# DeltaNet and expert layers on one core: first expert layer in 64-column tiles, and twelve unread products

## The chip, the core and the metric

The kernel runs on one core of one Trainium2 chip. The metric is the device time of one execution in microseconds, lower is better. [...] PEld is TensorE's weight load, DVE is VectorE, ACT ScalarE, POOL GpSimd, SP SyncE.

## What is computed

A DeltaNet recurrence over 4 batches, 8 heads and 768 steps of 48 values gives 3072 rows of 384 values. A gate gives each row one of 8 experts; each expert keeps its 80 rows of largest gate weight and sends them through two layers. The part around the change:

```python
logits = x @ w_gate                      # x: 3072 x 384, 8 experts
expert_idx = np.argmax(logits, axis=1)
...
for e in range(E):
    tok_idx = np.where(expert_idx == e)[0]
    if len(tok_idx) > capacity:          # capacity 80
        gw = gate_w[tok_idx]
        tok_idx = tok_idx[np.argpartition(-gw, capacity)[:capacity]]
    h = np.maximum(x[tok_idx] @ w1[e], 0.0)          # 384 -> 1024
    out[tok_idx] = gate_w[tok_idx, None] * (h @ w2[e])   # 1024 -> 384
```

Everything is float32, apart from a few bfloat16 helpers.

## The kernel before

The recurrence is cut into 12 chunks of 64 steps. For each chunk c a hand-written order runs on all engines: transposes of keys and queries (both), Gram products (gram), the inverse of a triangular matrix (solve, spread, merge_p2 to merge_y5), the state's chain (chain_ks, chain_tr, chain_qs, chain_ku, chain_pu), the transposes of the chunk's output rows (out_t, L500) and the gate's logits (logits, L510). Nearly all its products go through the helper mm (L207), so the profile shows them on one line and the tiles tell them apart: SB,KQ is chain_ks and chain_qs, R,Y chain_tr, UB,PT chain_pu, S_ps chain_ku, XB,B merge_p2. The products of chain_ks and merge_p2 take 128 rows by 64 columns of weights, and consecutive ones write the lower and the upper 64 partitions of the same PSUM tile in turn. The products with identb and eyes at L374 (128x128 weights, 512 columns of bfloat16) begin each merge_p2.

Behind the last chunk VectorE finds the 80 best rows of each expert (L598 to L837), helped by a few products, and writes the row numbers idx_g. GpSimd then gathers each expert's rows (gather, L849) into xgs[e], 80 rows by 384.

The expert part is plain code without a hand-written order: the framework's scheduler sets the order of its instructions on each engine, and it may set some of them among those of the recurrence's last chunks. For each expert e:

- tokens_in(e) (L858, L860) turns the gathered rows with three transposes into xTs[e], 128 x 3 x 80.
- First layer (L873): 8 blocks f of 128 hidden values, each the sum of 3 products over c, with 128x128 weights from w1_t and the 80 columns of xTs[e]. Four blocks share a PSUM tile hp; when its 12 products are done, ScalarE writes Relu of it into hT (L876).
- The next expert's tokens_in.
- Second layer (L881): 8 products of 128x80 weights from hT with 384 columns of w2_t, summed in yp.
- VectorE scales yp by the gate weight (L884), GpSimd scatters the rows to the output (L885).

A float32 product leaves two records in the trace, a transpose or a bfloat16 product one. Ten weight tiles (load_w, L152) are in SBUF at once, those of experts 0 to 4; expert e's two buffers are filled again for expert e + 5 when they come free.

## Time and profile before

| | |
|---|---|
| median of 3 runs | 464.94 us (463.93 to 469.27) |
| the profiled execution | 462.81 us |
| its span in the trace | 461.1 us |
| PE busy | 348.5 us (76% of the span) |
| PEld busy | 298.0 us (65%) |
| DVE, ACT, POOL busy | 234.1, 118.4, 167.0 us |
| L873, first expert layer, PE busy | 48.9 us, 384 records |
| L881, second expert layer, PE busy | 43.8 us, 128 records |

Times inside the profile are microseconds from the span's start. A busy PE counts overlapping records once; the distance between the starts of two groups tells how long the first one held the engine. The mean of one record is its latency, longer than its share of the engine. The recurrence ends at about 310 us, the choice of rows at about 358, the expert part runs from 363.6 us.

### The profile page before, as it was taken

What the parts mean: (1) busy time and instruction counts of PE and PEld (TensorE: products, weight loads), DVE (VectorE), ACT (ScalarE), POOL (GpSimd) and SP (SyncE); (2) the same over time, 40 slices, a digit from 0 to 9 for tenths busy, and PEclk for the clock granted to TensorE, in tenths of its full rate; (3) what the DMA queues carried; (4) which work ended last, traced back from release to release, by engine and by line L of the source; (5) the groups of instructions that cost most, each with busy time, mean ns of one, the idle gap of its engine ahead of it and who ended that gap; (6) DMA issues with size and microseconds to landing.
All of it is one profiled execution on the core that took longest, in us unless ns stands there. A gap on an engine that the chain in (4) does not pass through costs nothing. (4 is left out here: it accounts for less than half of the span.)

```text
span 461.1 us, 16603 instructions
## 1 busy us (share of the span) xinstructions
PE 348.5 (76%) x7239; PEld 298.0 (65%) x7239; DVE 234.1 (51%) x620; ACT 118.4 (26%) x208; POOL 167.0 (36%) x414
## 2 busy tenths in 40 slices
PE   2781688889898979897899998860002499999995
PEld 2671577688787878886788887750001477777773
DVE  6999861733646464765824864278598100110000
ACT  3410224424534353343352423510000000000000
POOL 5771170377374828581837341011000600011000
PEclk9975687999999999899999999995555569999999
DMA  9691566584857576774747345128399638940000
GB/s 156 121 180 35 100 111 129 84 192 82 190 106 171 106 170 124 156 157 84 163 77 178 51 115 118 43 86 302 125 372 414 240 129 278 300 162 12 21 12 11
DMA packets 183592, 65.30 MB, mean 142 GB/s; under 512 B 165568, under 2 KB 176832, under 8 KB 183520
## 3 DMA queue, kind: packets, MB, share of 16 engines
q1 hardware_dynamic: 135552, 54.36, 46.0%
q10 hardware_dynamic: 47200, 7.91, 9.4%
q0 software_dynamic: 768, 1.97, 1.4%
q8 instruction: 57, 0.93, 0.8%
q14 instruction: 15, 0.12, 0.1%
HBM read 44.35 MB, written 19.86 MB: 139 GB/s over the span
## 5 line engine op out<-in xcount | busy, mean ns | idle before, releaser
L873 PEld LDWEIGHTS hp<-xTe,w 128*128 128x128 f32 x384 | 48.9, 210 | 2.5 <-issue 1.5
L873 PE MATMUL hp<-xTe,w 128*128 128x80 f32 x384 | 48.9, 293 | 0.1
L345 POOL TENSOR_TENSOR tmpTrue<-XY,NT 128x14 f32<-128x14 f32 (+6 forms) x140 | 39.9, 285 | 11.0
L881 PE MATMUL yp<-w,hT 128*80 128x384 f32 x128 | 43.8, 497 | 0.0
L876 ACT ACTIVATE hT<-hp 128x320 f32<-128x320 f32 x16 | 7.0, 437 | 135.4 <-PE hp L873 135.4
L340 POOL TENSOR_TENSOR XY<-NT,eye 128x256 f32<-128x256 f32 x10 | 8.5, 853 | 91.2 <-DMA NT<-a_blocks 91.2
L347 POOL TENSOR_TENSOR XY<-XY,tmpTrue 128x14 f32<-128x14 f32 (+6 forms) x140 | 37.3, 266 | 11.0
L885 POOL DMA_INDIRECT out_dram<-y,idx_s x8 | 7.4, 920 | 81.7 <-DVE y L884 81.7
L207 PE MATMUL pm<-SB,KQ 128*64 128x96 f32 x704 | 34.6, 252 | 1.9 <-DVE lg L512 1.7
L303 ACT COPY KQ<-pm 128x512 f32<-128x512 f32 x48 | 24.9, 612 | 33.7 <-DMA a_blocks<-B 20.5
L454 DVE TENSOR_TENSOR UB<-pm,beta_t 64x768 f32<-64x768 f32 x24 | 22.9, 955 | 20.1 <-PE pm L207 19.8
L884 DVE TENSOR_SCALAR y<-yp,gw_t 80x384 f32<-80x384 f32 x8 | 4.9, 614 | 55.0 <-PE yp L881 55.0
L207 PEld LDWEIGHTS pm<-SB,KQ 128*64 128x64 f32 x704 | 30.7, 139 | 2.9 <-PE pm L591 2.0
L881 PEld LDWEIGHTS yp<-w,hT 128*80 128x80 f32 x128 | 19.1, 154 | 20.1 <-issue 20.1
L381 DVE TENSOR_TENSOR P<-pm,mask 128x512 f32<-128x512 f32 x24 | 15.4, 682 | 31.0 <-PE pm L207 31.0
L207 PE MATMUL pm<-KQ 48*64 48x128 f32 x768 | 25.8, 285 | 5.7 <-ACT KQ L303 3.8
L207 PE MATMUL pm<-YB,P 128*64 128x128 f32 x384 | 25.7, 288 | 3.4 <-issue 3.4
L207 PEld LDWEIGHTS pm<-KQ 48*64 48x64 f32 x768 | 22.3, 140 | 8.5 <-ACT KQ L303 4.8
L207 PEld LDWEIGHTS pm<-XB,B 128*64 128x64 f32 x384 | 22.3, 144 | 8.2 <-issue 7.7
L207 PE MATMUL pm<-XB,B 128*64 128x128 f32 x384 | 25.3, 288 | 2.6 <-DMA XB<-inv_blocks 2.6
L476 ACT COPY SB<-S_ps 48x768 f32<-48x768 f32 x22 | 17.4, 793 | 30.9 <-PE S_ps L207 30.7
L207 PEld LDWEIGHTS pm<-YB,P 128*64 128x64 f32 x384 | 22.4, 143 | 4.2 <-issue 3.6
(169 smaller groups left out, 648.5 us busy)
## 6 DMA issues: line engine op xcount, KB each, us to landing
w<-in_moe_w_dram SPq DMA_DIRECT2D x16, 1536.0 KB, 7.0
a_blocks<-B ACTq DMA_DIRECT2D x24, 256.0 KB, 4.8
qn<-in_q_dram SPq DMA_DIRECT2D x24, 192.0 KB, 5.1
vin<-in_v_dram SPq DMA_DIRECT2D x24, 192.0 KB, 6.0
x_rows<-x SPq DMA_DIRECT2D x24, 192.0 KB, 2.7
out_dram<-zero SPq DMA_DIRECT2D x12, 384.0 KB, 4.3
kr<-in_k_dram SPq DMA_DIRECT2D x23, 192.0 KB, 4.5
inv_blocks<-XY SPq DMA_DIRECT2D x12, 256.0 KB, 4.5
```

The source lines that it names most:

```text
L207: nc.tensor.matmul(out, lhsT=lhsT, rhs=rhs, start=not acc, stop=not acc, skip_group_check=True)
L303: nc.scalar.copy(KQs[c][:, 4 * h : 4 * h + 4, n, :], pt[:, h].rearrange("r (g w) -> r g w", w=128))
L340: eng.tensor_tensor(out=X, in0=NT.rearrange("p s t -> p t s"), in1=eye16, op=Alu.add)
L345: eng.tensor_tensor(out=tv, in0=X[:, t + 1 :, t : t + 1].to_broadcast(sh), in1=NT[:, 0:t, t].unsqueeze(1).to_broadcast(sh), op=Alu.mult)
L347: eng.tensor_tensor(out=X[:, t + 1 :, 0:t], in0=X[:, t + 1 :, 0:t], in1=tv, op=Alu.add)
L381: nc.vector.tensor_tensor(out=P2[:, p].rearrange("r g e w -> r (g e) w"), in0=ps[:, p].rearrange("r (g w) -> r g w", w=64), in1=mask.unsqu ...
L454: nc.vector.tensor_tensor(out=UB[hs(e), :, e].rearrange("r (g c) d -> r c g d", c=2), in0=ps[hs(e), :, : 8 * D].rearrange("r c (g d) -> r ...
L476: nc.scalar.copy(SB[hs(p, D), :, :, p].rearrange("r (b g) e d -> r b (g e) d", b=2), S_ps[hs(p, D), :, : 8 * D].rearrange("r b (g d) -> r ...
L873: nc.tensor.matmul(hp[:, (f - f0) * cap : (f - f0 + 1) * cap], lhsT=w1_t[:, c, f * 128 : (f + 1) * 128], rhs=xTs[e][:, c, :], start=(c == ...
L876: nc.scalar.activation(hT[:, f0:f1, :], hp[:, : (f1 - f0) * cap].rearrange("p (f t) -> p f t", t=cap), Act.Relu)
L881: nc.tensor.matmul(yp[:cap, :DM], lhsT=hT[:, f, :], rhs=w2_t[:, f, :], start=(f == 0), stop=(f == FK - 1))
L885: nc.gpsimd.indirect_dma_start(out=out[:, :], out_offset=bass.IndirectOffsetOnAxis(ap=idx_s[:, e : e + 1], axis=0), in_=y[:, :], element_o ...
```

## The change

The first layer's products are cut in two: each block of 128 hidden values is now two products with 64 columns of weights, one for the lower and one for the upper 64 partitions of hp, in turn, with the same 80 columns of tokens. The arithmetic is the same. And between the gathers and tokens_in(0) stand twelve products of identb with eyes, 512 columns of bfloat16, into a PSUM tile of the pool ps_y that nothing reads.

```diff
     for e in range(E):
         gather(e)
+    wm = ps_y.tile([128, 512], F32, name="yp")
+    for _ in range(12):
+        nc.tensor.matmul(wm, lhsT=identb, rhs=eyes.rearrange("r g w -> r (g w)"), start=True, stop=True)
     tokens_in(0)
     for e in range(E):
         w1_t, w2_t = w_t[2 * e], w_t[2 * e + 1]
...
             for f in range(f0, f1):
                 for c in range(DK):
-                    nc.tensor.matmul(hp[:, (f - f0) * cap : (f - f0 + 1) * cap],
-                                     lhsT=w1_t[:, c, f * 128 : (f + 1) * 128], rhs=xTs[e][:, c, :],
-                                     start=(c == 0), stop=(c == DK - 1))
+                    for n in range(2):
+                        r = slice(64 * n, 64 * n + 64)
+                        nc.tensor.matmul(hp[r, (f - f0) * cap : (f - f0 + 1) * cap],
+                                         lhsT=w1_t[:, c, f * 128 + 64 * n : f * 128 + 64 * n + 64], rhs=xTs[e][:, c, :],
+                                         start=(c == 0), stop=(c == DK - 1), skip_group_check=True)
```

Three lines are added above it, so in the changed kernel the unread products are L866, the first layer L878, the second L886.

On PE, at the end of the recurrence (L510 are the logits of chunk 10, the two groups of L207 chain_ks and chain_tr of chunk 11), the difference of the two orders reads, from the last of the first six unread products on:

```order
+L866 LDWEIGHTS identb
+L866 MATMUL yp<-eyes,identb 128x512
 L510 MATMUL pm<-wg,xT 64x8 x12
 L591 MATMUL pm<-ident,ohg 48x128
 L207 MATMUL pm<-SB,KQ 64x96 x16
-L207 MATMUL pm<-R,Y 64x48 x32
+L866 LDWEIGHTS identb
+L866 MATMUL yp<-eyes,identb 128x512
```

Six unread products stand between L500 of chunk 10 and L510, four behind chain_ks, then one product with R, two unread products, and the other 31 with R. None stands behind these.

On PE, where the choice of rows ends (L825) and the experts begin, before the change:

```order
L825 MATMUL acc<-rhs,hot 80x40
L858 MATMUL xp<-ident,xg 128x80 x6
L873 MATMUL hp<-xTe,w_5718 128x80 x24
L881 MATMUL yp<-w_5720,hT 80x384 x8
L873 MATMUL hp<-xTe,w_5722 128x80 x24
L858 MATMUL xp<-ident,xg 128x80 x3
L881 MATMUL yp<-w_5724,hT 80x384 x8
```

The same place now:

```order
L825 MATMUL acc<-rhs,hot 80x40
L858 MATMUL xp<-ident,xg 128x80 x6
L878 MATMUL hp<-xTe,w_5718 64x80 x48
L886 MATMUL yp<-w_5720,hT 80x384 x8
L878 MATMUL hp<-xTe,w_5722 64x80 x48
L858 MATMUL xp<-ident,xg 128x80 x3
L886 MATMUL yp<-w_5724,hT 80x384 x8
```

The first layer has 48 products of 64 columns of weights where 24 of 128 stood; between L825 and L858 nothing was added. The order on the other engines is the same as before.

## Rows read from the trace of the kernel before

**Rows 1.** Page, the span in 40 equal slices, busy tenths.

```profile
PE   2781688889898979897899998860002499999995
PEclk9975687999999999899999999995555569999999
```

**Rows 2.** Order of time on PE, expert part: start, busy us, group of records.

```profile
364.73 10.53 PE L873 MATMUL hp<-xTe,w 128*128 128x80 f32 x48
375.05 6.54 PE L881 MATMUL yp<-w,hT 128*80 128x384 f32 x16
381.43 5.48 PE L873 MATMUL hp<-xTe,w 128*128 128x80 f32 x48
386.75 0.37 PE L858 MATMUL xp<-ident,xg 80*128 80x80 f32 x3
386.96 5.33 PE L881 MATMUL yp<-w,hT 128*80 128x384 f32 x16
392.12 5.48 PE L873 MATMUL hp<-xTe,w 128*128 128x80 f32 x48
...
450.88 5.33 PE L881 MATMUL yp<-w,hT 128*80 128x384 f32 x16
```

**Rows 3.** Costliest groups, expert part: count, busy us, mean ns, idle before.

```profile
L873 PEld LDWEIGHTS hp<-xTe,w 128*128 128x128 f32 x384 | 48.9, 210 | 2.5 <-issue 1.5
L873 PE MATMUL hp<-xTe,w 128*128 128x80 f32 x384 | 48.9, 293 | 0.1
...
L876 ACT ACTIVATE hT<-hp 128x320 f32<-128x320 f32 x16 | 7.0, 437 | 135.4 <-PE hp L873 135.4
```

**Rows 4.** Order of time on PE, recurrence at full clock.

```profile
278.33 0.61 PE L374 MATMUL pm<-eyes,identb 128*128 128x512 bf16 x2
278.87 1.97 PE L207 MATMUL pm<-XB,B 128*64 128x128 f32 x32
280.77 0.88 PE L500 MATMUL pm<-ident,x 128*128 128x128 f32 x6
...
283.30 1.52 PE L207 MATMUL pm<-SB,KQ 128*64 128x96 f32 x32
284.75 1.14 PE L207 MATMUL pm<-P,YB 64*64 64x32 f32 x64
```

**Rows 5.** Stretches in which the granted clock rises (PEclk behind the engines).

```profile
52.00:54.00 2.00, 1.37 (x14) 0.98 (x10) 1.76 (x9) 2.00 (x5) 0.00 (x0) 0.69 0.72 68
...
76.00:78.00 2.00, 2.00 (x20) 1.78 (x18) 0.00 (x0) 1.13 (x3) 0.00 (x0) 0.72 0.02 8
...
377.00:378.00 1.00, 1.00 (x4) 0.50 (x3) 0.00 (x0) 0.00 (x0) 0.00 (x0) 0.75 0.79 250
```

**Rows 6.** Order of time on PE, the groups ahead of the first two rises.

```profile
49.70 3.67 PE L207 MATMUL pm<-XB,B 128*64 128x128 f32 x32 [2.02 <-DMA XB<-inv_blocks]
...
71.44 2.80 PE L207 MATMUL S_ps<-UB,kn 128*48 128x96 f32 x32 [2.11 <-DVE UB L454]
73.99 2.81 PE L207 MATMUL pm<-UB,PT 128*64 128x96 f32 x32
```

**Rows 7.** Order of time, PE and DVE, end of chunk 10 and chunk 11.

```profile
296.32 0.88 PE L500 MATMUL pm<-ident,x 128*128 128x128 f32 x6
...
298.34 0.87 PE L510 MATMUL pm<-wg,xT 128*64 128x8 f32 x24 [1.15 <-ACT xT L502]
...
299.37 1.54 PE L207 MATMUL pm<-SB,KQ 128*64 128x96 f32 x32
...
301.57 0.31 PE L207 MATMUL pm<-R,Y 64*64 64x48 f32 x2 [0.66 <-DVE R L442]
...
303.23 1.94 DVE L454 TENSOR_TENSOR UB<-pm,beta_t 64x768 f32<-64x768 f32 x2 [1.25 <-PE pm L207]
```

**Rows 8.** Stretches: PE, PEld, DVE, ACT, POOL busy, clock, DMA share, GB/s.

```profile
310.00:320.00 10.00, 0.10 (x5) 0.04 (x1) 8.68 (x40) 0.00 (x0) 0.84 (x3) 0.63 0.79 274
...
371.00:372.00 1.00, 1.00 (x6) 1.00 (x6) 0.00 (x0) 0.00 (x0) 0.00 (x0) 0.50 0.00 0
```

## The prediction

> **What bounds the kernel now.** I read the page's slices first [rows 1]. TensorE is busy for nine tenths or more of slices 33 to 39 (11.5 us each), behind a gap, and its granted clock is 0.5 from slice 28 into slice 33 (the mean of 0.63 at 310 to 320 us puts the fall at 312.6 [rows 8]). [...] Then the order of time on PE [rows 2]: an expert is 48 records of the first layer (L873; each float32 product leaves two records), 3 transposes for the next expert, 16 records of the second layer (L881), and the next begins at once: 392.12 - 381.43 = 10.69 us each. The last group ends at 450.88 + 5.33 = 456.2 us, then 4.9 us of scaling, scatter and closing follow, which the change leaves alone. No PE group of rows 2 shows idle time before it, so what PE saves here goes to the end one for one.

> At full clock the first layer takes 386.75 - 381.43 = 5.32 us, 110.8 ns a record, the second 392.12 - 386.96 = 5.16 us, 322 ns a record of 384 columns, 0.84 ns a column. By that the 80 columns of a first-layer record need 67 ns. They take 110.8 because weight loads are the limit: the load row has the same 48.9 us busy as the product row [rows 3].

> **First layer in two 64-column tiles.** 384 records become 768, with the same 80 columns against half the weights. The trace has this form: 128x64 weights, columns of float32, consecutive products alternating between the two halves of the output partitions (merge_p2, chain_ks). There [rows 4] 32 records of 128 columns take 280.77 - 278.87 = 1.90 us, 32 of 96 columns 284.75 - 283.30 = 1.45 us: 0.44 ns a column and record, half the 0.84 of one tile (0.42). So the two tiles do stream side by side, and the loads lie under the streams. With 0.42 a column, the 96-column group leaves 1.45 - 32 x 96 x 0.00042 = 0.16 us over. If that is paid once a group, an expert's 96 records take 96 x 80 x 0.00042 + 0.16 = 3.39 us; if it is paid by record (5 ns), 3.71. I take 3.5, since the 128-column group leaves about the same 0.18 over. Bounds: 3.23 with nothing over, and 96 x 45.3 = 4.35 us if a record with 80 columns costs what one with 96 does. Gain: 5.32 - 3.5 = 1.82 us in each of experts 1 to 7, 12.7 us.

> [...]

> What hides the rest: ScalarE's Relu of the second half, 437 ns [rows 3], is needed only by the fifth product of the second layer, behind the transposes and four products (0.2 and 2.6 us), so it isn't late; without that cover it would cost half a us an expert. Weights: no DMA moves anything at 371 us [rows 8], so the ten tiles of experts 0 to 4 are in; the other six are issued when a buffer comes free, five experts before they are read, some 44 us ahead at the new pace. They aren't late next either; one that were would cost PE its remaining flight.

> **Expert 0 and the clock.** It takes 381.43 - 364.73 = 16.70 us now, 10.32 for the first layer, all at 0.5, and 6.38 for the second. The clock rose at 377.5 [rows 5], 2.4 us after the second layer began; 10.3 us of L873 before it had not raised it. What raised it elsewhere [rows 5, 6]: a group of 128x64 tiles from 49.70 on (rise at 53.2, 3.5 us later), and two such groups, of 48 and 64 columns, from 71.44 on (rise at 77.1, 5.7 us later). The new first layer has the form of these groups, so I expect the rise inside it, from 3.5 us after its start to its end at 6.4; between the two rows lies 4.6, and I take 4.7. At the half clock a record of 96 columns took 2.55 us / 32 = 80 ns (from 71.44 to the next group at 73.99 [rows 6], and 0.84 x 96 = 81); with 80 columns 67 ns. So 4.7 us hold 70 records, the other 26 take 0.95 us at 36.5 ns: 5.65, then 5.16 for the second layer at full clock. 16.70 - 10.81 = 5.9 us gained.

> **The twelve unread products.** They do not run while the rows come: the order places them ahead of that, six between the transposes of chunk 10 (L500) and its logits (L510), four behind chunk 11's first products (SB,KQ), two behind the first product with R. Ahead of the experts PE waits as it did, and the clock, which fell at 312.6 with the recurrence over, is not held up by products at 297 to 303 us. What they cost: two of the same shape took 278.87 - 278.33 = 0.54 us with the change of tiling [rows 4], 0.27 each at most. Now [rows 7]: PE is done with L500 at 297.2; six take 1.6 us, to 298.8, where L510 began at 298.34: 0.5 late. The SB,KQ group starts 0.5 late and takes 1.45; four more take 1.1 us, while the first R product waited until 2.20 after SB,KQ's start: 0.3 late. Two more take 0.5 where the wait for the second R was already under way: 0.2 to 0.4 late. Sum of the small delays 0.9 to 1.2; with the products at 0.22 (512 columns at half of 0.84, bfloat16 streaming at twice float32's rate) about 0.6. I take 0.8. Bounds: 0.3, and all of it, 12 x 0.27 = 3.2. Behind the waiting R product stand chunk 11's remaining products and, on VectorE, UB at 303.23, from which VectorE works on with hardly a gap (8.68 of 10 us at 310 to 320 [rows 8]) to the indices of the gather. So this delay moves the whole end.

> **Sum.** 12.7 + 5.9 - 0.8 = 17.8 us off the profiled execution's 462.81 (span 461.1 and 1.7 around it): 445.0. The median of the runs shown is 464.94, 2.1 more than the profiled one; I go half way, and forecast **446.0 us**.

> **Rivals.**
> 1. The clock rises only with the second layer, as now. For: in 10.3 us of L873 it didn't. Against: rows 6. Then 96 x 67 ns = 6.4 and 6.38 us, 2.0 more: 448.0.
> 2. The products cost their whole length, 3.2 instead of 0.8, because each change of tiling adds to them. For: three stretches in the middle of 64-column groups. Against: two of them stand where PE waited anyway. 448.4.
> 3. A record of 80 columns costs what one of 96 does, 45.3 ns. For: no row has 80 columns. 4.35 us an expert, 0.97 x 7 = 6.8 us; expert 0 gains 5.1 (59 records of 80 ns, 37 of 45.3, and 5.16); with -0.8 that is 11.1: 452.8.
> 4. [...] A 64-column load is 110.8 / 2 = 55.4 ns, a stream 67 ns; in series on each of two tiles 61 ns a record, 5.88 us an expert: 7 x 0.56 = 3.9 lost, 1.4 more in expert 0 (11.8 us at the half clock, no early rise), 0.8 for the products: 470.0. It decides from 55 ns a record at full clock. Against: rows 4 (59 ns with 128 columns, where the series would be 81), and L873 itself, whose 110.8 already hides a 67 ns stream.

> [...]

> **How the numbers follow.** Forecast 0.63, rival 1 0.13, rival 2 0.07, rival 3 0.10: all faster by over 1%, 0.93. A record of 53 to 55 ns, between rivals 3 and 4, would end within 1% (about what a measurement of this kernel can tell from no change): 0.03. Rival 4: 0.04. The range reaches from 442.5 (3.3 us an expert, 14.1 in seven; rise after 3.5 us, 6.5; products at 0.3: 20.3 us off the profiled execution, with no addition for the median) to 453.5, which takes in rivals 1 to 3.

> **What would show it.** Right: in the order of time, first-layer groups of 96 records, 3.4 to 3.7 us to the next group; experts 8.9 us apart; the granted clock rising inside the first group of the new tiles, before the second layer; the products at 297 to 303 us, UB of chunk 11 about 0.8 us later, and the gather's start later by the same. Wrong: groups of over 5.3 us (rival 4), a first group of 6.4 us at 0.5 throughout (rival 1), UB 3 us late (rival 2), experts more than 9.6 us apart (rival 3), or PE idle before a second layer, waiting for Relu or weights, which I have priced at nothing.

## The result, and the profile after

| | before | after |
|---|---|---|
| median | 465.42 us (463.93 to 469.27, 4 runs) | 448.47 us (445.92 to 448.77, 4 runs) |
| profiled execution | 462.81 us | 448.49 us |
| its span | 461.1 us | 446.7 us |

The ratio is 0.9611, with a 95% interval from 0.9543 to 0.968: faster, 2.5 us above the forecast of 446.0 and inside the range. The experiments further down ran beside runs of the kernel before on the same chip (17, 7 and 11); the 17 spread from 461.7 to 471.2 us, so parts of a microsecond are read from the traces and not from the times. Medians are of all executions; ratios leave out the slow ones, those more than 1.5% above the fastest of the same kernel (one of the 11 took 708 us).

The two lines of the page that answer to [rows 1], in 40 slices of now 11.2 us (PE is TensorE; PEclk is its granted clock in tenths of full speed, which stands at 0.5 or at 1.0 in the traces of before and after, a slice with both showing the mean):

```profile
PE   2752696889898989888979989897000148999995
PEclk9976688999999989999999999899555559999999
```

The low stretch of the clock is still there, over 5 slices instead of 5 and a part, and the dense end behind it is shorter. The order of time on PE in the expert part, against [rows 2] (start, busy us, group):

```profile
366.91 3.55 PE L878 MATMUL hp<-xTe,w 128*64 128x80 f32 x54
370.78 0.37 PE L878 MATMUL hp<-xTe,w 128*64 128x80 f32 x4 [0.32 <-issue]
371.50 0.23 PE L878 MATMUL hp<-xTe,w 128*64 128x80 f32 x1 [0.34 <-issue]
372.22 1.51 PE L878 MATMUL hp<-xTe,w 128*64 128x80 f32 x37 [0.49 <-issue]
373.66 5.39 PE L886 MATMUL yp<-w,hT 128*80 128x384 f32 x16
378.98 3.59 PE L878 MATMUL hp<-xTe,w 128*64 128x80 f32 x96
...
388.01 3.54 PE L878 MATMUL hp<-xTe,w 128*64 128x80 f32 x96
391.49 0.43 PE L858 MATMUL xp<-ident,xg 80*128 80x80 f32 x3
391.75 5.33 PE L886 MATMUL yp<-w,hT 128*80 128x384 f32 x16
397.00 3.54 PE L878 MATMUL hp<-xTe,w 128*64 128x80 f32 x96
...
436.44 5.39 PE L886 MATMUL yp<-w,hT 128*80 128x384 f32 x16
```

An expert takes 397.00 - 388.01 = 8.99 us where it took 10.69: the first layer 391.49 - 388.01 = 3.48 instead of 5.32, the transposes 0.26 instead of 0.21, the second layer 397.00 - 391.75 = 5.25 instead of 5.16. Expert 0 takes 378.98 - 366.91 = 12.07 instead of 16.70, with a pause in it: PE had done 54 of 96 records and did next to nothing from 370.3 to 372.2, waiting for no semaphore ("issue"). The clock rose at 369.9 us, 2.9 after the start of the layer, as the mean of 0.57 (third value from the end) over this microsecond gives it:

```profile
369.00:370.00 1.00, 1.00 (x22) 1.00 (x20) 0.00 (x0) 0.00 (x0) 0.78 (x1) 0.57 0.44 123
```

The end of chunk 10 and chunk 11, against [rows 7]:

```profile
297.71 0.88 PE L500 MATMUL pm<-ident,x 128*128 128x128 f32 x6
298.43 1.46 PE L866 MATMUL yp<-eyes,identb 128*128 128x512 bf16 x6
...
299.81 0.87 PE L510 MATMUL pm<-wg,xT 128*64 128x8 f32 x24
...
300.84 1.54 PE L207 MATMUL pm<-SB,KQ 128*64 128x96 f32 x32
302.31 1.04 PE L866 MATMUL yp<-eyes,identb 128*128 128x512 bf16 x4
303.28 0.31 PE L207 MATMUL pm<-R,Y 64*64 64x48 f32 x2
303.52 0.60 PE L866 MATMUL yp<-eyes,identb 128*128 128x512 bf16 x2
304.06 1.14 PE L207 MATMUL pm<-R,Y 64*64 64x48 f32 x62
...
305.26 1.94 DVE L454 TENSOR_TENSOR UB<-pm,beta_t 64x768 f32<-64x768 f32 x2 [1.81 <-PE pm L207]
```

The twelve products run at 298.4 to 304.0 us, none of them in the wait for the rows. From L500's start to UB it is 7.55 us, before it was 6.91: they cost 0.64. But L500 itself began 1.39 us later than before, though the two orders are the same up to there. The last 1.7 us of that came between the L500 of chunk 9 (0.27 us earlier than before) and that of chunk 10, and two stretches show where, by the clock in the kernel before and after:

```profile
288.00:292.00 4.00, 3.65 (x118) 3.34 (x119) 2.01 (x3) 1.65 (x3) 0.00 (x0) 1.00 0.03 8
```

```profile
288.00:292.00 4.00, 4.00 (x77) 3.74 (x73) 1.91 (x2) 0.00 (x0) 0.00 (x0) 0.58 0.08 28
```

In this execution the clock was at its lower level for most of these four microseconds. Such short falls come in the recurrence at changing places (the granted clock was 0.5 from 189.8 to 193.2 us in the kernel before, and from 161.6 to 165.1, 233.3 to 236.7 and 287.9 to 291.3 in the changed one), so nothing ties this one to the change. With them the recurrence drifts: L500 of chunk 6 began 3.4 us earlier than before.

**The account of the profiled executions.** Experts 1 to 7: 456.21 - 381.43 = 74.78 us before, 441.83 - 378.98 = 62.85 after, 11.93 gained. Expert 0: 4.63 gained. The products: 0.64 lost. The start of chunk 10's end: 1.39 lost. From UB to the first layer: 0.15 lost. Sum 14.4, the difference of the spans. The 1.39 are where the recurrence happened to stand in these two executions; in another pair of executions the difference of the spans can be another by some microseconds.

### The profile page after: what moved, and what is told of

It reads as the page before. It is cut to its first block, busy times and chain, and to the rows that moved or that the text cites. A ratio compares the mean times of both kernels' runs of the same rounds, so it can differ in the third digit from the quotient of the medians.

```text
span 446.7 us, 17395 instructions
## 1 busy us (share of the span) xinstructions
PE 334.0 (75%) x7635; PEld 279.6 (63%) x7635; DVE 234.7 (53%) x620; ACT 118.4 (27%) x208; POOL 167.3 (37%) x414
## 5 line engine op out<-in xcount | busy, mean ns | idle before, releaser
L886 PE MATMUL yp<-w,hT 128*80 128x384 f32 x128 | 42.7, 487 | 0.0
L881 ACT ACTIVATE hT<-hp 128x320 f32<-128x320 f32 x16 | 7.0, 437 | 118.8 <-remote 61.3
L207 PE MATMUL pm<-SB,KQ 128*64 128x96 f32 x704 | 34.6, 252 | 1.7 <-DVE lg L512 1.7
L878 PEld LDWEIGHTS hp<-xTe,w 128*64 128x64 f32 x768 | 28.7, 142 | 6.1 <-issue 6.1
L207 PEld LDWEIGHTS pm<-SB,KQ 128*64 128x64 f32 x704 | 30.6, 139 | 2.6 <-PE pm L591 2.0
L878 PE MATMUL hp<-xTe,w 128*64 128x80 f32 x768 | 30.5, 240 | 1.3 <-issue 1.2
L886 PEld LDWEIGHTS yp<-w,hT 128*80 128x80 f32 x128 | 18.5, 150 | 19.5 <-issue 19.3
L207 PE MATMUL pm<-KQ 48*64 48x128 f32 x768 | 25.9, 285 | 5.9 <-ACT KQ L303 4.8
L207 PE MATMUL pm<-YB,P 128*64 128x128 f32 x384 | 28.4, 306 | 1.6 <-issue 1.6
L207 PEld LDWEIGHTS pm<-KQ 48*64 48x64 f32 x768 | 22.4, 140 | 8.4 <-ACT KQ L303 5.5
L207 PEld LDWEIGHTS pm<-XB,B 128*64 128x64 f32 x384 | 22.1, 143 | 8.6 <-issue 8.6
L207 PE MATMUL pm<-XB,B 128*64 128x128 f32 x384 | 24.9, 285 | 3.0 <-DMA XB<-inv_blocks 3.0
L207 PEld LDWEIGHTS pm<-YB,P 128*64 128x64 f32 x384 | 24.9, 155 | 2.8 <-issue 2.1
```

The lines of the kernel that those rows point to most:

```text
L207: nc.tensor.matmul(out, lhsT=lhsT, rhs=rhs, start=not acc, stop=not acc, skip_group_check=True)
L878: nc.tensor.matmul(hp[r, (f - f0) * cap : (f - f0 + 1) * cap], lhsT=w1_t[:, c, f * 128 + 64 * n : f * 128 + 64 * n + 64], rhs=xTs[e][:, c, :],
L881: nc.scalar.activation(hT[:, f0:f1, :], hp[:, : (f1 - f0) * cap].rearrange("p (f t) -> p f t", t=cap), Act.Relu)
L886: nc.tensor.matmul(yp[:cap, :DM], lhsT=hT[:, f, :], rhs=w2_t[:, f, :], start=(f == 0), stop=(f == FK - 1))
```

## Experiments

My theory was: all the gain is the 64-column tiles', in their pace and in an earlier rise of the clock in expert 0, and the pace comes from two tiles that stream at once. Rivals: the unread products help; or the shorter weight loads are all, in whatever order; or a 64-column product streams at twice the speed by itself.

**Each part alone.** The two parts were built apart: the tiles without the three lines of unread products, the products with the first layer of before, and both once more.

> Only the 64-column tiles of the first layer, no unread products. My theory: all of the gain is the tiles', and the products cost 0.6 us on the way to VectorE's UB of chunk 11. So experts 1 to 7 stand 9.0 us apart as in the changed kernel, the granted clock rises inside the first layer of expert 0, and the time is 0.6 us below the changed kernel's on the same chip (ratio to before 0.958 to 0.962). Rival: the products help the clock or the pace; then this kernel is at least 1 us slower than the changed one. On the pause of 2 us in expert 0's first layer (PE stopped after 54 of 96 records, with no semaphore to wait for): if PE ran out of instructions at a fixed place of its stream, the 24 instructions taken out move it 12 records on, to record 66; if it comes from the gathers or the clock's change, it stays about 3.4 us behind the start of that layer.

> Only the twelve unread products, the first layer with 128 columns of weights as before. My theory: they run at about 298 to 304 us and cost 0.6 us: 0.3 to 1.0 us slower than before, ratio 1.000 to 1.003; experts 10.69 us apart, the clock rises 2.4 us or so into the second layer of expert 0 as before. Rival: they keep the clock up or raise it sooner: 1 to 3 us faster than before.

> The changed kernel once more, to compare with the others on one chip: ratio 0.959 to 0.964 to before. If the pause of 2 us in expert 0's first layer belongs to PE's stream it stands after record 54 again; if it was a chance event of that execution it is gone or elsewhere.

| | median us | ratio to before, 95% interval |
|---|---|---|
| tiles_only | 449.18 (7 runs) | 0.9641 (0.9592 to 0.9689) |
| products_only | 466.19 (12 runs) | 0.9973 (0.9927 to 1.0019) |
| both_again | 449.59 (6 runs) | 0.9591 (0.9521 to 0.9662) |
| before, beside them | 465.76 (17 runs) | |

The tiles alone give the gain; the products alone change nothing that the times can show. My expectations for the products, 0.6 us lost in both pairs, aren't borne out by the times: by the ratios the kernels with the products are 1.3 us (products_only against before) and 2.3 us (both_again against tiles_only, 0.9591 and 0.9641) faster, by the medians 0.4 slower, and neither is clear of the noise. In the trace of products_only:

```profile
301.31 0.87 PE L500 MATMUL pm<-ident,x 128*128 128x128 f32 x6
...
308.73 1.54 PE L207 MATMUL pm<-SB,KQ 128*64 128x96 f32 x32
...
370.50 10.53 PE L876 MATMUL hp<-xTe,w 128*128 128x80 f32 x48
380.82 6.50 PE L884 MATMUL yp<-w,hT 128*80 128x384 f32 x16
```

From L500 to the group behind the R products it is 308.73 - 301.31 = 7.42 us, the same in the changed kernel (305.13 - 297.71), and in the kernel before, where that group began at 303.10, 6.78: again 0.64 for the products. The expert part is as before (10.3 us for the first layer of expert 0). So the products don't help the experts. Whether they help where they stand is open: in tiles_only the clock fell for 3.4 us just there (304.4 to 307.8), and the same stretch took 309.66 - 301.51 = 8.15 us, 1.37 more than before; in none of the three traces with the products did it fall there. In ten traces without them it happened four times (tiles_only, late_products, late_products_20, by_half: the SB,KQ group there took 2.4 to 2.8 us instead of 1.54); too few to say that they prevent it.

Expert 0 in tiles_only has no pause:

```profile
372.73 5.14 PE L875 MATMUL hp<-xTe,w 128*64 128x80 f32 x96
377.80 5.39 PE L883 MATMUL yp<-w,hT 128*80 128x384 f32 x16
```

```profile
374.00:376.00 2.00, 2.00 (x36) 2.00 (x34) 0.00 (x0) 0.00 (x0) 1.21 (x2) 0.50 0.31 93
376.00:378.00 2.00, 2.00 (x53) 1.91 (x50) 0.00 (x0) 0.52 (x2) 0.00 (x0) 0.98 0.25 70
```

5.07 us, with the rise at 376.1 us, 3.4 after the layer's start. both_again has none either: its first layer takes 376.09 - 370.12 = 5.97 us, the rise 5.2 after the start. So the pause belonged to one execution, at no fixed place of PE's stream, and neither of the two places that I had named.

**The products where they were meant to stand.** One small product of gw_t ahead of them, into the same PSUM tile, ties them to the end of the choice of rows; the order then has all of them between L825 and L858. late_products keeps twelve, late_products_20 has twenty, as in the diff.

```diff
     wm = ps_y.tile([128, 512], F32, name="yp")
+    nc.tensor.matmul(wm[:E, :E], lhsT=gw_t, rhs=gw_t, start=True, stop=True)
-    for _ in range(12):
+    for _ in range(20):
```

> The changed kernel with one small product of the gate weights ahead of the twelve, into the same PSUM tile, so that the order places all of them behind the choice of rows, in the wait for the gathered rows. My theory: twelve times 0.43 us at the half clock fill about 360.4 to 365.6 us, the transposes of expert 0 start no more than 0.3 us later, and the clock rises before the first layer of expert 0 or in its first 1.5 us. That layer then takes 3.5 to 4.5 us where it took 6.75 with the pause (5.2 if the pause stays): 1 to 2.5 us faster than tiles_only. Rival: the rise comes from the first layer alone; then this is equal to tiles_only or 0.3 us slower.

> Twenty unread products instead of twelve behind the choice of rows, in the wait for the gathered rows. With twelve the clock rose at 363.1, PE then waited 1.8 us for the rows, and the clock fell again at 366.5, as the first layer began. My theory: twenty leave no such wait, the clock stays up, and expert 0's first layer takes 3.5 us instead of 5.1; where the clock rises late they hold back the transposes by up to 2 us. Sum between 1.6 faster and 1 slower than with twelve. Rival: the clock falls all the same, because these products don't hold it: first layer 5 us or more, and the time the same or up to 2 us slower.

With twelve, 447.98 us, ratio 0.9613 (0.9553 to 0.9673):

```profile
358.63 4.96 PE L867 MATMUL yp<-eyes,identb 128*128 128x512 bf16 x12
365.40 0.60 PE L858 MATMUL xp<-ident,xg 80*128 80x80 f32 x6 [1.80 <-issue]
366.30 5.19 PE L879 MATMUL hp<-xTe,w 128*64 128x80 f32 x96 [0.29 <-DVE xTe L860]
```

```profile
364.00:366.00 2.00, 0.60 (x6) 0.48 (x6) 0.16 (x1) 0.00 (x0) 1.39 (x3) 1.00 0.33 108
366.00:368.00 2.00, 1.71 (x29) 1.70 (x30) 0.56 (x2) 0.00 (x0) 1.58 (x2) 0.63 0.42 121
```

They did raise the clock, at 363.1. Then PE had nothing for 1.8 us, and the clock fell again at 366.5, just behind the first layer's start: 5.11 us for that layer (the second began at 371.41), as good as the 5.07 of tiles_only. My number for it, 3.5 to 4.5, failed by this second fall, and the time can't be told from that of tiles_only. With twenty, 447.64 us, ratio 0.9572 (0.9473 to 0.9671):

```profile
365.68 6.60 PE L867 MATMUL yp<-eyes,identb 128*128 128x512 bf16 x20
372.12 0.58 PE L858 MATMUL xp<-ident,xg 80*128 80x80 f32 x6
373.00 3.54 PE L879 MATMUL hp<-xTe,w 128*64 128x80 f32 x96 [0.29 <-DVE xTe L860]
376.47 5.39 PE L887 MATMUL yp<-w,hT 128*80 128x384 f32 x16
```

```profile
370.00:372.00 2.00, 2.00 (x11) 0.93 (x10) 0.00 (x0) 0.00 (x0) 1.39 (x3) 1.00 0.29 84
```

The transposes follow on the products at once, the clock stays up, and the first layer takes its full-clock 3.47 us. From the first L825 group to expert 1's first layer this is 381.78 - 362.21 = 19.57 us; in tiles_only 383.11 - 361.57 = 21.54. Of these 2 us 1.60 are the first layer's, 0.26 the transposes', which stand at full clock now, and 0.11 lie ahead of them. Whether the products hold the transposes back this pair can't tell: from the first L825 group to the transposes it took 9.9 to 10.4 us in the three traces with late products, and 8.5 to 8.8 or 9.6 to 10.3 in the ten others, tiles_only with 10.02. In the medians, whose intervals overlap, the gain isn't settled.

**What the pace of the tiles comes from.** Four forms without the products, one run each. In by_half the loop over n stands outside the one over c (three products of the lower half, then three of the upper), in half_runs outside the one over f too (twelve and twelve); quarter_tiles has four tiles of 32 columns in turn; one_tile sends five of six products to the lower tile:

```diff
+                        if c < DK - 1:
+                            r = slice(0, 64)
                         nc.tensor.matmul(hp[r, (f - f0) * cap : (f - f0 + 1) * cap],
```

> The 64-column tiles without the unread products, but the three products of the lower half first and then the three of the upper half, so that consecutive products use the same tile. My theory: the gain is that two tiles stream at once, which needs products in turn; here a record costs about the 67 ns of its own stream (80 columns at 0.84 ns), less where the tile changes, so 4.5 to 6.4 us for 96 records at full clock where 3.48 were measured, up to the 5.32 of before or above. Rival: it is the shorter weight load alone, in whatever order: 3.5 us again.

> The first layer in four tiles of 32 columns in turn, without the unread products. My theory: the streams set the pace, and four at once carry the same columns a microsecond: 192 records of 17.5 to 19 ns, 3.4 to 3.7 us an expert, the time of the 64-column tiles. [...]

> The 64-column form without the unread products, but five of every six products go to the lower tile and one to the upper (the upper half of h then holds a third of its sum, the lower half too much): as many records, the same loads and streams. Theory A: a tile streams at 0.84 ns a column and the gain comes from two tiles at once, also where several products of one tile stand in a row (by_half took 3.66 us, so PE must start the other tile's products early). Then ten of twelve records share one tile, 80 x 67 ns = 5.4 us an expert at full clock. Theory B: a product with 64 columns of weights streams at 0.42 ns a column by itself, on whatever tile: 3.5 us, as in turn.

> The 64-column form without the unread products, 12 products (24 records) of the lower tile in a row, then 12 of the upper. Theory A, with PE running ahead by some records only: 24 of a tile are too many to overlap fully, 4.5 to 6.4 us an expert; if it runs ahead by more than 24 records, 3.5 to 4. Theory B: 3.5 us.

Expert 1 in by_half, in one_tile, in half_runs and in quarter_tiles; from the first row to the transposes is one first layer at full clock:

```profile
379.93 3.73 PE L875 MATMUL hp<-xTe,w 128*64 128x80 f32 x96
383.59 0.43 PE L858 MATMUL xp<-ident,xg 80*128 80x80 f32 x3
```

```profile
378.67 5.75 PE L877 MATMUL hp<-xTe,w 128*64 128x80 f32 x96
384.35 0.42 PE L858 MATMUL xp<-ident,xg 80*128 80x80 f32 x3
```

```profile
379.50 6.19 PE L875 MATMUL hp<-xTe,w 128*64 128x80 f32 x96
385.62 0.43 PE L858 MATMUL xp<-ident,xg 80*128 80x80 f32 x3
```

```profile
376.79 3.53 PE L875 MATMUL hp<-xTe,w 128*32 128x80 f32 x192
380.25 0.43 PE L858 MATMUL xp<-ident,xg 80*128 80x80 f32 x3
...
391.50 0.61 PE L875 MATMUL hp<-xTe,w 128*32 128x80 f32 x19 [2.49 <-issue]
```

| | us for an expert's first layer | time of the run |
|---|---|---|
| in turn (after) | 3.48 | 448.49 |
| by_half, 6 records a tile | 3.66 | 450.63 |
| half_runs, 24 records a tile | 6.12 | 467.45 |
| one_tile, 10 of 12 records on one | 5.68 | 463.50 |
| quarter_tiles, 192 records | 3.46 | 449.97 |

My expectation for by_half (4.5 or more) was wrong, and it looked like the rival: with six records of a tile in a row it is only 0.18 us slower. one_tile and half_runs decide against that rival. With the same loads and the same number of streams, ten of twelve records on one tile take 5.68 us, near 80 x 67 ns = 5.4; and 24 records in a row take 6.12 us, 64 ns a record, nearly the 67 of one stream. So a 64-column product has no speed of its own. The starts of the single records show how PE passes from tile to tile: in half_runs records of one tile start 69 ns apart at full clock, and when three of the 24 are still to start, the other tile's begin between them; so at all 24 changes of tile within an expert. Three records ahead are enough to keep both tiles at work in runs of six (38 ns a record), and cover only a small part of runs of 24 (64 ns). Four tiles give the same 3.46 us: the streams, not the records, set the pace (18 ns a record). The series of rival 4 in the prediction, load and stream of a tile one behind the other (122 ns a record), is excluded too: the 80 records on one tile in one_tile take 5680 / 80 = 71 ns each.

**The second layer in the same form.** The pace suggests it: 16 records of 384 columns with only 80 columns of weights take 5.25 us. Here w2 gives the weights and the 80 tokens are the stream; the result is transposed and has to be turned back.

```diff
+            for f in range(FK):
+                for n in range(2):
+                    r = slice(64 * n, 64 * n + 64)
+                    nc.tensor.matmul(ypT[e][r, c * cap : (c + 1) * cap],
+                                     lhsT=w2_t[:, f, c * 128 + 64 * n : c * 128 + 64 * n + 64], rhs=hT[:, f, :],
+                                     start=(f == 0), stop=(f == FK - 1), skip_group_check=True)
...
+        nc.vector.tensor_copy(yT, ypT[e][:, : DK * cap].rearrange("p (c t) -> p c t", c=DK))
+        for c in range(DK):
+            nc.tensor.transpose(yp[:cap, c * 128 : (c + 1) * 128], yT[:, c, :], ident)
```

> Without the unread products; the second layer too in 64-column tiles: weights from w2, the 80 tokens of hT as the stream, the result transposed in PSUM, copied by VectorE, turned back by three transposes behind the next expert's first layer, then scaled as before. By the pace measured for the first layer (3.48 us for 96 records) the second takes 3.5 instead of 5.25, six transposes 0.5: an expert 7.4 to 7.7 us instead of 8.99, 10 to 12 us off tiles_only less about 1 for the longer end: 437 to 441 us, ratio to before 0.94 to 0.95. Rival: the Relu of the second half is no longer covered, or the weights come too late: PE idle before the second layer, 8.3 us an expert or more.

> Both layers in 64-column tiles, and twenty unread products behind the choice of rows in the wait for the gathered rows. By second_tiles (439.8) and the 1.1 to 1.6 us that the clock gave late_products_20 in expert 0's first layer: 437 to 440 us, ratio to before 0.938 to 0.946; expert 0's first layer 3.5 us. Rival: the products hold the transposes back by as much as the clock gives: the same as second_tiles, 0.944.

second_tiles (L888 is the first layer, L901 the second, L869 the transposes back):

```profile
377.03 3.49 PE L888 MATMUL hp<-xTe,w 128*64 128x80 f32 x96
380.45 0.43 PE L858 MATMUL xp<-ident,xg 80*128 80x80 f32 x3
380.71 0.49 PE L869 MATMUL yp<-ident,yT 128*80 128x128 f32 x3
381.14 3.54 PE L901 MATMUL hp<-hT,w 128*64 128x80 f32 x96
384.51 2.79 PE L888 MATMUL hp<-xTe,w 128*64 128x80 f32 x74
387.97 0.99 PE L888 MATMUL hp<-xTe,w 128*64 128x80 f32 x22 [0.67 <-issue]
```

384.51 - 377.03 = 7.48 us an expert, as expected, without the stops that some experts have (the last row; see the end), and neither Relu nor a weight tile makes PE wait there. 439.78 us, ratio 0.944 (0.9314 to 0.9565). With the twenty late products as well it is 435.02 us (432.07 to 439.67, 6 runs) against 464.46 before, ratio 0.9384 (0.9315 to 0.9453): the fastest version of all, faster than both kernels of this study, and below the 437 to 440 us that I had expected (the ratio is inside). How much of the step from 0.944 to 0.938 the products give, the overlapping intervals leave open: expert 0's first layer takes 367.12 - 363.75 = 3.37 us there and 373.50 - 369.06 = 4.44 without them.

## Why the prediction was right

**The bound and its lever.** "What PE saves here goes to the end one for one" held: the experts' 16.6 us reach the end without a new wait behind them, and what is missing of them in the 14.4 was lost ahead of the experts; Relu and weights, priced at nothing, cost nothing.

**The pace of the tiles.** Forecast 3.5 us a first layer, measured 3.48. The two tiles stream at once, as the groups of [rows 4] had shown (0.44 ns a column and record against 0.84); one_tile (5.68 us) and half_runs (6.12) are what shows it. Mis-sized were the neighbours, for which I had taken no change: the transposes and the second layer behind the first grew by 0.05 and 0.09 us, so seven experts gained 11.9 us and not 12.7. What makes them grow, no run shows.

**Rival 4** (slower) fell at 36 ns a record where it needed 55, and where nearly all records stand on one tile (one_tile) each takes 71 ns, near its stream's 67 and far from the 122 of stream and load in series.

**Expert 0.** Forecast: the rise 4.7 us into the first layer and 5.65 us for it. Measured rises at 2.9, 3.4 and 5.2 us after its start in three executions, and without the pause 5.07 and 5.97 us for the layer. The step held, and rival 1 (no rise before the second layer) fell in each of them, while in products_only, with the layer of before, the rise came in the second layer again. The forecast's earliest rise, 3.5 us, was too late: in the five other traces with a tiled first layer and no products in the wait it came 2.2 to 4.4 us after the start, in one_tile and half_runs too (4.4 and 2.2), whose pace at full clock is no faster than before. So the rise doesn't hang on the gain in pace; what in the tiled form brings it about, no run shows. The 1.3 us that expert 0 took beyond the forecast are, as an estimate, the pause of about 1.9 less what the early rise gave.

**The products.** That they stand ahead of the wait and do not hold the clock up to the experts was right; the cost, forecast at 0.8, was 0.64 in the traces, and rival 2 fell. The 0.22 us that I took for a product of 512 bfloat16 columns, at twice float32's rate, is what the trace shows: within the first six they start 216 ns apart, 0.42 ns a column where float32 takes 0.84. Behind the last of each of the three groups the next product starts after 309 ns, 93 more; how much of that the change of tiling is, no run shows.

**The sum.** 17.8 us were forecast, 14.4 came in the profiled execution: 0.8 from the experts' neighbours, 1.3 in expert 0, 1.4 from the recurrence, which stood later by chance in this execution, 0.15 in the way of the rows, 0.16 back from the products (3.45 with two places each). Among the thirteen traces L500 of chunk 10 began at anything from 293.8 to 302.2 us, so that the sum and the median come this close to the forecast is in part luck; what the traces bear out closely is the expert part. Rival 3's experts, more than 9.6 us apart, were not seen.

## What to carry to other kernels

Where a product's stream is shorter than what its weight load lets through, as read here from 110.8 ns a record for a stream of 67, with the load row as busy as the product row, halving the weights into two column tiles paid (3.48 us a first layer instead of 5.32), because the streams of the two tiles run at once; price it as columns times the pace of one tile, divided by the number of tiles (3.23 us for two tiles and for four, measured 3.48 and 3.46), and add what a group took beyond that (0.16 us in [rows 4], 0.25 here) and the 0.14 by which its neighbours grew. Keep the tiles in turn: six records of one tile in a row cost 0.18 us an expert, 24 lost all of the gain (6.12 us). And look up where a scheduler puts work that depends on nothing: the twelve products stood at 298 to 304 us, over 60 us ahead of the experts that the code has behind them. What is meant to bridge a wait is best tied to the wait's beginning and made to reach to its end: twelve products left PE 1.8 us without work and the clock fell, twenty left none and it stayed up.

## What the hardware showed that I had not expected

```profile
387.00:388.00 1.00, 0.33 (x10) 0.17 (x6) 0.00 (x0) 0.00 (x0) 0.00 (x0) 1.00 1.00 386
```

  The DMA engines were full here (1.00, the value before the last), but idle at the 0.64 us of quarter_tiles. The trace points to a late supply of instructions. Queue q8 brings them 16 KB at a time: 60 packets, 0.98 MB on the page of the changed kernel ("q8 instruction"), whose 7635 records of products and as many of loads make about 255 a packet. The stops of second_tiles stand about 128 product records apart, so 256 with the loads, and each of the seven in the three kernels ended 1.3 to 1.4 us behind the landing of such a packet. No run tested it. The stop in expert 0 of the changed kernel is another: no packet of q8 landed between 311.7 and 374.8 us, and its cause stays open.
